# One block of a fused scan and feed-forward kernel moved from per-pair to joint processing

## The chip, the core and the metric

The kernel runs on one core of a Trainium2 chip. A core has five engines that run side by side and wait for each other through semaphores: TensorE (PE, matrix products; its weight loads are shown as PEld), VectorE (DVE), ScalarE (ACT), GpSimd (POOL) and SyncE (SP, which here only issues transfers). SP, ScalarE and GpSimd can each issue transfers (DMAs) between the device memory and the on-chip memory. TensorE writes to eight on-chip accumulator banks (PSUM); VectorE and ScalarE read them, GpSimd does not. The metric is the device time of the whole kernel in microseconds; lower is better.

## The reference

A state-space scan over 4 sequences of 768 tokens, 8 heads of 32 values and 16 states, and then a bilinear feed-forward of 3,072 tokens:

```
for each chunk of the sequence (log_a, cum: decay within the chunk)
    M = (C @ B^T) * exp(cum_i - cum_j) * causal       # per head, tokens by tokens
    y = M @ x  +  (C @ state) * exp(cum)              # within the chunk, and from before it
    state = decay * state + sum_j exp(cum_end - cum_j) * B_j x_j
X   = y laid out as (3072 tokens, 256)
out = ((X @ w_a) * (X @ w_b)) @ w_out                 # 256 -> 1536 -> 256
```

Inputs and outputs are float32; the kernel multiplies in float16 and accumulates in float32.

## The kernel before, in words

**Tiling.** The 768 tokens of a sequence are cut into 6 blocks of 128. The 4 sequences form 2 pairs, so there are 12 steps, called pair 0 to pair 11: pairs 0 and 1 are block 0, pairs 2 and 3 are block 1, and so on. A pair holds two sequences (`bt`), 256 tokens.

**One pair's scan.** Its B, C and x are loaded (`load1`, `load2`). `scale_bc` multiplies B and C by decay factors, `scale_x` scales x to float16. B and C are turned so that the state index lies on the partitions: for pairs 0 to 3 by TensorE (`transposes`, with copies BT by ScalarE and CT by VectorE), for later pairs by a transposing transfer (`turn`, which SP issues after GpSimd has filled `planes`). `scores` writes C times B into the four banks SC0 and SC1. `mask` multiplies each quarter by the causal triangle, on VectorE, or by way of a ScalarE copy `tmp` on GpSimd (`by_pool=True`). Then come the products with the incoming state (`Sbd`, made on GpSimd by `state_spread`), with x (`pv_u`), and the state sums (`ds_mm`), all in the SC banks again.

**Two forms of a block.** Pairs 0 to 3 run one by one: `pv` computes one pair's output into SC1 and copies it to `X2T`; its state product (line 492) takes the full, block-diagonal `sbd` of 128 x 512, spread with `maskbd`. From pair 4 on, a block runs jointly: `group` and `outputs` compute both pairs' outputs (state product at line 523 with the small `spair`), and three ScalarE copies (lines 551 and 553) write them to `XB`.

**Feed-forward.** A per-pair unit (`unit_mm`, line 616) covers two of the 12 slices of 128 hidden columns for 256 tokens: four matmuls of 256 columns into a bank for `aps`, four into a bank for `bps`. ScalarE copies aps to `asb` (`evac_a`, line 630), VectorE multiplies bps and asb (`times`, line 637). A joint unit (`bunit`, line 682) covers one slice for the 512 tokens of a block: two matmuls of 512 columns for each. The output product (`out_mm` at line 652, `bout` at line 709) takes 12 matmuls for each 128 tokens; ScalarE copies the result (`osb`), SP stores it.

**Order.** The order is written by hand (`manual_schedule`): each engine runs its instructions in the order of the Python calls, and so does each queue of transfers. In the built program a transfer also waits until the one eight places before it on the same issuer has landed. A matmul's first write to a bank waits until the bank's last reader is done. The feed-forward and output tiles share four banks; the string `BANKS` says which bank each tile takes, in order of the calls.

**Around the change.** GpSimd issues, one after another, the weight loads (`load_w`, `load_wo`) and some inputs of pairs 1 and 2; SP issues B, C and x of pair 3 after the second half of Wb has landed (`w1[1]`), then those of later pairs and the transposing loads. PE interleaves block 0's units with the scan of pairs 1, 2 and 3, then block 1's units pair by pair, and joins the joint form at block 2 (line 682 for the first time at 52.20 us).

Of the kernel before, what the change touches and what calls it, by code (L numbers as in the profile page):

```python
# [22 lines left out]
    "032130132013201320120310231023120132031203120132013201320310213021320310231023120130231023"  # L23
    "1021320312031203123021302130213021302130213021031203120312031203120312031203120312031"
# [4 lines left out]
def kernel(  # L29
# [26 lines left out]
    NG = NBLK - 1  # L56
    P0 = 4
# [10 lines left out]
    ph = np.zeros((128, H + 2), np.float32)  # L68
    ph[:, 0:H] = (j[:, None] // N) == np.arange(H)[None, :]
    ph[:, H:] = (j[:, None] // N) % 2 == np.arange(2)[None, :]  # L70
# [4 lines left out]
    ch = const.tile([128, H + 2], f32, name="ch")  # L75
# [5 lines left out]
    headm = ch[:, 0:H]  # L81
    par = ch[:, H:]
# [8 lines left out]
    X2T = big.tile([128, P0, 2, 2, Q], f16, name="X2T")  # L91
    XB = big.tile([128, NBLK - P0 // NBP, 2, 2, NBP, Q], f16, name="XB")
    U32 = big.tile([128, NP, 2, 2 * D], f32, name="U32")
    gU = big.tile([128, NP, 2, 2 * D], f32, name="gU")
    maskbd = big.tile([128, H, D], f16, name="maskbd")
# [92 lines left out]
    nc.sync.dma_start(ch, ph_t.ap())  # L188
# [240 lines left out]
    def pv_u(p, u, py, first):  # L429
# [12 lines left out]
        for r in range(2) if p < P2 else ():  # L442
            for g in range(4):
                for bt in range(2):
                    h = u * 4 + g
                    k = slice(64 * bt, 64 * bt + 64)
                    c0 = 32 * (g ^ 2 * bt) if p >= P0 else 32 * g
                    nc.tensor.matmul(  # L448
                        py[bt, u][c0 : c0 + 32] if p >= P0 else py[bt][c0 : c0 + 32, u * Q : (u + 1) * Q],
                        s["X16"][k, h, r, :],  # L450
                        s["T1"][k, h, r, :],
                        start=(first and u == 0 and r == 0),
                        stop=(r == 1),
                        skip_group_check=True,
                        tile_position=(64 * bt, c0),
                    )
# [28 lines left out]
    def pv(p, DS=None, split=False):  # L485
        blk, bp = divmod(p, NBP)
        s = st[p]
        PY = [SC1[:, bt, 0:256] for bt in range(2)]
        if blk > 0:
            for bt in range(2):  # L490
                for u in range(2):
                    nc.tensor.matmul(
                        PY[bt][:, u * Q : (u + 1) * Q],
                        s["Sbd"][:, bt, u * 128 : u * 128 + 128],
                        s["CT"][:, bt],
                        start=(u == 0),
                        stop=False,
                        skip_group_check=True,
                    )
        for u in range(2):  # L500
            pv_u(p, u, PY, blk == 0)
        if blk < NBLK - 1:
            ds_mm(p, *(DS or (256, SC[2:])))
        o_ = X2T[:, p].rearrange("p t u q -> p t (u q)")
        i_ = SC1[:, :, 0:256]
        if split:
            c0 = nc.scalar.activation(out=o_[:, 0], in_=i_[:, 0], func=AF.Copy, scale=YS / XS)
            c1 = nc.vector.tensor_scalar(o_[:, 1], i_[:, 1], YS / XS, None, ALU.mult)
            tc.declare_no_dep(c1.ins, c0.ins.name, reason="reads of two banks")
        else:  # L510
            nc.scalar.activation(out=o_, in_=i_, func=AF.Copy, scale=YS / XS)

    def outputs(blk):
# [29 lines left out]
        for bt, to, fr in ((0, whole, whole), (1, low, high), (1, high, low)):  # L543
            if blk == NBLK - 1:
                for j in range(NBP):
                    o_ = XB[to, blk - P0 // NBP, :, bt, j]
# [7 lines left out]
                out=XB[to, blk - P0 // NBP, :, bt].rearrange("p u j q -> p u (j q)"),  # L554
# [29 lines left out]
    def state_spread(p):  # L584
        blk, bp = divmod(p, NBP)
        if p + NBP < P0:
            Sbd = mid.tile([128, 2, H * D], f16, name="sbd", tag="sbd")
            nc.gpsimd.tensor_tensor(
                out=Sbd.rearrange("p t (m c) -> p t m c", m=4),
                in0=U32[:, p].unsqueeze(2).broadcast_to((128, 2, 4, 2 * D)),  # L590
                in1=maskbd.rearrange("p (m e) d -> p m (e d)", e=2).unsqueeze(1).broadcast_to((128, 2, 4, 2 * D)),
                op=ALU.mult,
            )
        else:
            Sbd = mid.tile([128, 2, 2 * D], f16, name="spair", tag="spair")
            nc.gpsimd.tensor_tensor(
                out=Sbd.rearrange("p t (e d) -> p t e d", e=2),
                in0=U32[:, p].rearrange("p t (e d) -> p t e d", e=2),
                in1=par.unsqueeze(1).unsqueeze(3).broadcast_to((128, 2, 2, D)),
                op=ALU.mult,  # L600
            )
# [72 lines left out]
    def bunit(blk, k):  # L674
# [4 lines left out]
        for W in (Wa, Wb):  # L679
            t_ = bank("aps" if W is Wa else "bps")  # L680
            for f in range(2):
# [5 lines left out]
                    XB[:, blk - P0 // NBP, f].rearrange("p t j q -> p (t j q)"),  # L687
# [12 lines left out]
    def bout(blk, c, parts=1):  # L700
# [4 lines left out]
        for part in range(parts):  # L705
# [16 lines left out]
            if blk * NBP < P2:  # L722
# [99 lines left out]
    for bt in range(2):  # L822
        load1(nc.gpsimd, 2, 1, bt)
    load_wo(0)
    nc.gpsimd.tensor_copy(maskbd, headm.unsqueeze(2).broadcast_to((128, H, D)))
    load_wo(1)
    tiles(3)
    for bt in range(2):
        load1(nc.gpsimd, 2, 2, bt)
    times(0, 0, bps[0], asb[0])  # L830
    pv(1, DS=(0, SC[:2]), split=True)
# [6 lines left out]
    for t_ in planes:  # L838
        nc.gpsimd.memset(t_[:, 0:4].bitcast(u32), 0)
    scale_bc(2, 1, nc.gpsimd)  # L840
    go((1, 0), (1, 1), (1, 2))
    state_sums(0)
    state_sums(1)
    state_spread(0)
    state_spread(1)
    b3 = [load1(nc.sync, 3, 0, bt) for bt in range(2)]
    tc.add_manual_dep(b3[0].ins, w1[1].ins.name, AFTER, reason="weights ahead of pair 3's inputs")
    for bt in range(2):
        load1(nc.sync, 3, 1, bt)
    loads_x(3, nc.sync)  # L850
    loads_bc(4)
    go((0, 3), (0, 4), (1, 3), (0, 5))
    transposes(2, apart=True)
    go((1, 4))
    h = unit(1, 5)
    scores(2)
    mask(product(2, 3), by_pool=True)
    mask(product(2, 0))
    mask(product(2, 1))
    mask(product(2, 2))  # L860
    h()
    scale_x(2, nc.scalar)
    scale_bc(3, 0, nc.gpsimd)
    scale_bc(3, 1, nc.gpsimd)
    scale_x(3, nc.gpsimd)
    loads_bc(5)
    o = [bank("ops"), bank("ops")]
    out_mm(0, 0, o[0], range(6))
    out_mm(0, 1, o[1], range(6))
    out_mm(0, 0, o[0], range(6, NK))  # L870
    out_store(0, 0, o[0])
    pull(2)
    pv(2, split=True)
    out_mm(0, 1, o[1], range(6, NK))
    out_store(0, 1, o[1])
    h = unit(2, 0, lambda: transposes(3, apart=True))
    state_sums(2)
    fb(2)
    h()
    h = unit(2, 1)  # L880
# [46 lines left out]
    scores(3)  # L927
    prep(4, (2,))
# [5 lines left out]
    mask(product(3, 0))  # L934
    h()
    for m in range(1, 4):
        mask(product(3, m))
    out_half(1, 0)
    out_half(1, 1)
    go((2, 2))  # L940
    pull(3)
    pv(3)
    state_sums(3)
    late_rows(nc.gpsimd)
    state_spread(3)
    nc.gpsimd.tensor_copy(
        causal_r.rearrange("p r (s i) -> p r s i", s=2), causal.rearrange("p r (i s) -> p r s i", s=2)
    )
    go((2, 3), (2, 4), (2, 5))
    late_factors()  # L950
    fb(3)
    out_half(2, 0)
    o_ps = bank("ops")
    out_mm(2, 1, o_ps, range(6))
# [5 lines left out]
    masked(4, (0, 1))  # L960
    out_mm(2, 1, o_ps, range(6, NK))
    out_store(2, 1, o_ps)
    masked(4, (2,), *pu(3, 0))
    go((3, 1))
    scale_x(5, nc.scalar)
# [105 lines left out]
```

## Time and profile before

| | |
|---|---|
| median of 3 runs | 125.04 us (124.65 to 125.16) |
| span of the profiled execution | 123.5 us; what lies around it, against the median, 1.5 us |
| TensorE busy | 117.6 us, 95% of the span |
| VectorE, ScalarE, GpSimd busy | 86.4, 71.9, 62.8 us |
| granted TensorE clock | 1.00 throughout |
| transfers | 13.74 MB |

Times in the text count from the start of the span. Busy PE includes overlapped matmuls, so the cost of a piece is taken from the start of one piece to the start of the next. "L616" is line 616 of the kernel before; a helper's line stands for all its calls.

### The profile page before, as it was taken

The page shows a single profiled execution, that of the slowest core. Times are in us where ns is not written, and L with a number is a line of the kernel's source. Part 1 is how long each engine was busy: PE and PEld are TensorE (multiplying, and loading weights), DVE is VectorE, ACT ScalarE, POOL GpSimd, SP SyncE. Part 2 cuts the span into 40 slices and gives each one's busy share as a digit, 9 for nine tenths or more (in the row PEclk, how much of TensorE's full clock was granted, in tenths as well). Part 3 has the DMA queues.
Part 4 walks back from the last instruction along what each step waited for, and adds up shares of the span by engine and source line. Part 5 has one row for each costly group of instructions (what it writes and reads, how often), then busy time and mean ns, then how long its engine had stood idle before and what let it go on. Part 6 is the DMA issues. An engine that isn't in the chain of part 4 may idle for free.

```text
span 123.5 us, 3874 instructions
## 1 busy us (share of the span) xinstructions
PE 117.6 (95%) x1527; PEld 79.8 (65%) x1527; DVE 86.4 (70%) x166; ACT 71.9 (58%) x142; POOL 62.8 (51%) x109
## 2 busy tenths in 40 slices
PE   5988999999999999899999999999999999999990
PEld 2445698978898788644467455756464784655880
DVE  1886889795968979298984989857899444847100
ACT  0465845866364795687758746664737736566220
POOL 7999999956873399089850895026900000000000
PEclk9999999999999999999999999999999999999999
DMA  3999999994659988697995973999541012010132
GB/s 64 154 163 237 171 196 181 194 145 74 99 115 185 92 83 147 84 120 79 134 155 74 150 264 87 70 95 161 113 130 42 5 42 85 0 42 0 48 101 69
DMA packets 60754, 13.74 MB, mean 111 GB/s; under 512 B 55632, under 2 KB 60400, under 8 KB 60736
## 3 DMA queue, kind: packets, MB, share of 16 engines
q1 hardware_dynamic: 56608, 9.53, 49.8%
q0 software_dynamic: 2128, 3.61, 16.3%
q10 hardware_dynamic: 2000, 0.36, 1.6%
q8 instruction: 12, 0.20, 0.7%
q14 instruction: 6, 0.05, 0.1%
HBM read 11.13 MB, written 3.15 MB: 116 GB/s over the span
## 4 chain that ended last, share of the span: by engine, by line
PE 83%; DMA 6%; POOL 5%; ACT 2%; issue 1%; DVE 1%; ACTq 0%; POOLq 0%
PE ops L709 18%; PE aps L682 17%; PE bps L682 17%; PE ops L652 9%; PE aps L616 8%; PE bps L616 7%; DMA xn<-in_x_dram 6%; PE SC L373 2%; PE SC L448 1%; PE SC L433 1%; PE SC L388 1%; POOL cn L154 1%; PE SC L523 1%; PE SC L475 1%; POOL bn L154 1%; POOL causal L214 1%
## 5 line engine op out<-in xcount | busy, mean ns | idle before, releaser
L630 ACT COPY asb<-aps 128x512 f32<-128x512 f32 x72 | 41.9, 587 | 14.8 <-PE aps L682 9.7
L694 DVE TENSOR_TENSOR hkb<-bps,asb 128x512 f16<-128x512 f32 x48 | 32.3, 689 | 12.9 <-ACT asb L630 11.7
L682 PE MATMUL aps<-XB,Wa 128*128 128x512 f16 x96 | 28.6, 379 | 0.0
L682 PE MATMUL bps<-XB,Wb 128*128 128x512 f16 x96 | 28.5, 379 | 0.0
L709 PE MATMUL ops<-Wo,hkb 128*128 128x256 f16 (+1 forms) x204 | 22.5, 267 | 0.0
L709 PEld LDWEIGHTS <-hkb 128*128 128x128 f16 x204 | 18.5, 98 | 3.1
L637 DVE TENSOR_TENSOR hk<-bps,asb 128x512 f16<-128x512 f32 x24 | 16.2, 688 | 2.9 <-ACT asb L630 2.4
L682 PEld LDWEIGHTS <-Wb 128*128 128x128 f16 x96 | 9.9, 103 | 11.0 <-issue 0.2
L427 DVE TENSOR_TENSOR t<-SC,causal_q 128x512 f16<-128x512 f32 x21 | 13.4, 682 | 3.9 <-PE SC L373 3.9
L682 PEld LDWEIGHTS <-Wa 128*128 128x128 f16 x96 | 9.7, 103 | 9.1 <-issue 0.4
L616 PE MATMUL aps<-X2T,Wa 128*128 128x256 f16 x96 | 14.3, 273 | 0.4 <-DMA Wa<-in_moe_w_a_dram 0.3
L721 ACT ACTIVATE osb<-ops 128x256 f32<-128x256 f32 (+1 forms) x16 | 6.0, 377 | 14.3 <-PE ops L709 14.2
L616 PE MATMUL bps<-X2T,Wb 128*128 128x256 f16 x96 | 14.3, 273 | 0.0
L652 PE MATMUL ops<-Wo,hk 128*128 128x256 f16 x96 | 11.6, 273 | 0.0
L616 PEld LDWEIGHTS <-Wa 128*128 128x128 f16 x96 | 9.5, 103 | 2.0 <-DMA Wa<-in_moe_w_a_dram 0.8
L616 PEld LDWEIGHTS <-Wb 128*128 128x128 f16 x96 | 9.7, 103 | 0.7
L652 PEld LDWEIGHTS <-hk 128*128 128x128 f16 x96 | 8.9, 98 | 1.5 <-DVE hk L637 0.2
L293 POOL TENSOR_SCALAR x<-xn 128x512 f16<-128x512 f32 x6 | 9.0, 1493 | 1.7 <-DMA xn<-in_x_dram 1.3
L427 DVE TENSOR_TENSOR t<-SC,causal 128x512 f16<-128x512 f32 x13 | 8.2, 684 | 1.4 <-PE SC L388 1.3
L304 POOL TENSOR_TENSOR planes<-cn,fCl 128x256 f16<-128x256 f32 x6 | 3.7, 622 | 8.1 <-DMA cn<-in_C_dram 8.1
L425 POOL TENSOR_TENSOR t<-tmp,causal_q 128x512 f16<-128x512 f32 x3 | 3.5, 1159 | 7.3 <-ACT tmp L424 7.2
L553 ACT ACTIVATE XB<-SC 64x512 f16<-64x512 f32 (+1 forms) x9 | 5.3, 594 | 2.9 <-PE SC L462 1.6
(102 smaller groups left out, 128.8 us busy)
## 6 DMA issues: line engine op xcount, KB each, us to landing
out_dram<-osb SPq DMA_DIRECT2D x19, 128.0 KB, 1.8
xn<-in_x_dram SPq DMA_DIRECT2D x5, 256.0 KB, 5.3
xn<-in_x_dram SPq DMA_DIRECT2D x7, 128.0 KB, 3.4
Wa<-in_moe_w_a_dram POOLq DMA_DIRECT2D x2, 384.0 KB, 6.2
Wb<-in_moe_w_b_dram POOLq DMA_DIRECT2D x2, 384.0 KB, 7.8
Wo<-in_moe_w_out_dram POOLq DMA_DIRECT2D x2, 384.0 KB, 6.8
cn<-in_C_dram SPq DMA_DIRECT2D x6, 128.0 KB, 4.2
bn<-in_B_dram SPq DMA_DIRECT2D x6, 128.0 KB, 4.3
```

Source lines behind the costliest of these rows:

```text
L293: eng.tensor_scalar(xo, xi, XS, None, ALU.mult)
L304: eng.tensor_tensor(out=planes[p % 2][:, 4:6].rearrange("p t (h n) -> p t h n", n=N), in0=raw, in1=f.unsqueeze(3).broadcast_to((128, 2, H, ...
L427: nc.vector.tensor_tensor(out=o_, in0=i_, in1=c_, op=ALU.mult)
L553: nc.scalar.activation(out=XB[to, blk - P0 // NBP, :, bt].rearrange("p u j q -> p u (j q)"), in_=SCt[bt][fr, :, 0 : NBP * Q], func=AF.Copy ...
L616: nc.tensor.matmul(ps[:, kk * 2 * Q : (kk + 1) * 2 * Q], W[k // 6][:, f, k % 6 // 3 * 384 : (k % 6 // 3 + 1) * 384].rearrange("p (c kk) -> ...
L630: (nc.vector.tensor_copy if on_dve else nc.scalar.copy)(asb, a_ps)
L637: nc.vector.tensor_tensor(out=s["hk"][:, 2 * k2 : 2 * k2 + 2, :].rearrange("p k q -> p (k q)"), in0=b_ps, in1=asb, op=ALU.mult)
L652: nc.tensor.matmul(o_ps[:, 0:d_model], hk[:, k, bt * Q : (bt + 1) * Q], Wo[:, k, :], start=(k == 0), stop=(k == NK - 1), skip_group_check= ...
L682: nc.tensor.matmul(t_, W[k // 6][:, f, k % 6 // 3 * 384 : (k % 6 // 3 + 1) * 384].rearrange("p (c kk) -> p kk c", kk=3)[:, k % 3], XB[:, b ...
L694: return lambda: nc.vector.tensor_tensor(out=s["hk"][:, k], in0=ps[1], in1=asb, op=ALU.mult)
L709: nc.tensor.matmul(o_ps[:, 0:w], hk[:, k, c * Q : (c + 1) * Q], Wo[:, k, cs], start=(k == 0), stop=(k == NK - 1), skip_group_check=True,)
L721: nc.scalar.activation(out=o_sb[:, 0:w], in_=o_ps[:, 0:w], func=AF.Copy, scale=1.0 / (YS * YS))
```

## The change

Block 1 takes the joint form. `X2T` keeps two pairs (`PJ = 2`), `XB` holds five blocks, and `pv` shrinks to `pv1` for pair 1 alone. The block-diagonal `sbd`, `maskbd` and the head mask constant go. Pairs 2 and 3 are scored and masked one after the other among the last units and first output products of block 0; then `group(1)`, the rest of block 0's output products, and 12 joint units of block 1 around the scores of pairs 4 and 5. B and C of pair 3 are issued by GpSimd ahead of both halves of `Wo`, x of pairs 2 and 3 by SP after Wb's second half; the second half of `Wo` is issued after pair 2's B and C are scaled. `planes` are cleared later. x of pair 3 is scaled by ScalarE instead of GpSimd. Block 1's masks use GpSimd three times (before once). The results of block 1 join the late stores of block 0. `BANKS` is new.

```diff
+    PJ = 2
-    X2T = big.tile([128, P0, 2, 2, Q], f16, name="X2T")
-    XB = big.tile([128, NBLK - P0 // NBP, 2, 2, NBP, Q], f16, name="XB")
+    X2T = big.tile([128, PJ, 2, 2, Q], f16, name="X2T")
+    XB = big.tile([128, NBLK - PJ // NBP, 2, 2, NBP, Q], f16, name="XB")
-    maskbd = big.tile([128, H, D], f16, name="maskbd")
...
-    def pv(p, DS=None, split=False):
+    def pv1():
...
     for bt in range(2):
         load1(nc.gpsimd, 2, 1, bt)
+    tiles(3)
+    for w in range(2):
+        for bt in range(2):
+            load1(nc.gpsimd, 3, w, bt)
     load_wo(0)
-    nc.gpsimd.tensor_copy(maskbd, headm.unsqueeze(2).broadcast_to((128, H, D)))
-    load_wo(1)
-    tiles(3)
-    for bt in range(2):
-        load1(nc.gpsimd, 2, 2, bt)
+    for p in (2, 3):
+        for x_ in load2(nc.sync, p, 2):
+            tc.add_manual_dep(x_.ins, w1[1].ins.name, AFTER, reason="weights ahead of x")
+    loads_bc(4)
     times(0, 0, bps[0], asb[0])
...
     scale_bc(2, 0, nc.gpsimd)
-    for t_ in planes:
-        nc.gpsimd.memset(t_[:, 0:4].bitcast(u32), 0)
     scale_bc(2, 1, nc.gpsimd)
+    load_wo(1)
+    scale_bc(3, 0, nc.gpsimd)
+    scale_bc(3, 1, nc.gpsimd)
     go((1, 0), (1, 1), (1, 2))
     state_sums(0)
     state_sums(1)
+    for t_ in planes:
+        nc.gpsimd.memset(t_[:, 0:4].bitcast(u32), 0)
     state_spread(0)
     state_spread(1)
...
-    go((0, 3), (0, 4), (1, 3), (0, 5))
+    go((0, 3), (0, 4), (1, 3))
     transposes(2, apart=True)
-    go((1, 4))
-    h = unit(1, 5)
-    scores(2)
+    fb(2)
+    go((0, 5))
+    h = unit(1, 4, lambda: scores(2))
+    h()
     mask(product(2, 3), by_pool=True)
     mask(product(2, 0))
+    h5 = unit(1, 5)
+    transposes(3, [bank("tb"), bank("tc")])
+    mask(product(2, 2), by_pool=True)
     mask(product(2, 1))
...
     o = [bank("ops"), bank("ops")]
     out_mm(0, 0, o[0], range(6))
     out_mm(0, 1, o[1], range(6))
+    h5()
+    scores(3)
+    mask(product(3, 3), by_pool=True)
+    for m in range(3):
+        mask(product(3, m))
+    scale_x(2, nc.scalar)
+    for bt in range(2):
+        o.append(bank("ops"))
+        out_mm(1, bt, o[-1], range(6))
     out_mm(0, 0, o[0], range(6, NK))
+    scale_x(3, nc.scalar)
     out_store(0, 0, o[0])
+    loads_bc(5)
+    late_rows(nc.gpsimd)
...
+    prep(4)
     loads_x(4, nc.sync)
     loads_x(5, nc.sync)
     prep(5)
     loads_bc(6)
     loads_bc(7)
+    group(1)
+    for c in range(1, 4):
+        p, bt = divmod(c, NBP)
+        out_mm(p, bt, o[c], range(6, NK))
+        out_store(p, bt, o[c])
+    state_spread(2)
+    state_spread(3)
     late_factors()
     fb(3)
+    bgo(1, 0, 1, 2, 3)
     scores(4)
     mask(product(4, 3), by_pool=True)
     scale_x(4, nc.scalar)
     prep(6)
+    for m in range(3):
+        mask(product(4, m))
+        bgo(1, *range(4 + 3 * m, min(7 + 3 * m, NK)))
     scores(5)
     mask(product(5, 3), by_pool=True)
+    scale_x(5, nc.scalar)
...
+    for m in range(3):
+        mask(product(5, m))
+    bout(1, 0)
+    bout(1, 1)
     group(2)
-    out_half(3, 0)
-    out_half(3, 1)
+    bout(1, 2)
+    bout(1, 3)
```

## The prediction, made before the changed kernel was run

> **What bounds the kernel now.** I read the page first: who is busy, and the chain that ended last.
>
> ```profile
> PE 117.6 (95%) x1527; PEld 79.8 (65%) x1527; DVE 86.4 (70%) x166; ACT 71.9 (58%) x142; POOL 62.8 (51%) x109
> PEclk9999999999999999999999999999999999999999
> PE 83%; DMA 6%; POOL 5%; ACT 2%; issue 1%; DVE 1%; ACTq 0%; POOLq 0%
> L682 PE MATMUL aps<-XB,Wa 128*128 128x512 f16 x96 | 28.6, 379 | 0.0
> L616 PE MATMUL aps<-X2T,Wa 128*128 128x256 f16 x96 | 14.3, 273 | 0.4 <-DMA Wa<-in_moe_w_a_dram 0.3
> ```
>
> TensorE is the bound, at the full clock. The 379 and 273 ns are pipelined durations; the price of a matmul is the step from one start to the next, which the chain of waits shows. So I took the chain next, over the stretch that the change rewrites.
>
> ```profile
> 18.85 0.59 ACT asb L630
> 19.47 0.70 DVE hk L637
> 20.21 0.60 PE aps L616 x4
> ...
> 22.55 0.44 PE bps L616 x4
> ...
> 27.39 0.32 PE SC L492 x4
> 27.71 0.35 PE SC L448 x32
> ...
> 47.49 0.25 PE SC L523 x16
> 47.74 0.65 PE SC L448 x62
> 48.39 0.26 PE SC L475 x29
> 48.65 2.74 PE ops L652 x24
> 51.41 0.39 ACT osb L664
> 51.88 0.40 PE SC L373 x14
> ```
>
> A half unit (four 256-column matmuls) takes 0.44. The chain leaves TensorE once, at 18.85, until a bank is free at 20.21, and again at 51.4. In between it never leaves it: a gain here is PE work removed, and any new wait comes straight off it. After 52 us the order of work on PE is the same in both kernels, so I compare when the scores of pair 6 start (51.30 by the timeline).
>
> Last, the loads and the ScalarE step that could become new waits (timeline, and the list of issues over windows of a single issue):
>
> ```profile
> Wo<-in_moe_w_out_dram POOLq DMA_DIRECT2D x1, 384.0 KB, 7.5
> xn<-in_x_dram SPq DMA_DIRECT2D x2, 128.0 KB, 3.2
> 33.22 1.32 SPq L356 DMA_TRANSPOSE turned<-planes  x1
> 34.72 2.71 SPq L154 DMA_DIRECT2D xn<-in_x_dram  x4
> 41.42 0.63 ACT L291 ACTIVATE x<-xn 128x512 f16<-128x512 f32 x1
> ```
>
> The scale of pair 4's x (41.42) found its x long landed. In the changed kernel it comes some 4 us earlier.
>
> **The bank table: -0.25.** In before the first aps of (0,4) should follow at 19.09 + 2 x 0.437 = 19.96 but starts at 20.21, because its bank is that of (1,2)'s bps, read by VectorE until 20.16. In the new table that unit's aps takes the bank of (1,2)'s aps, copied out by 19.44, and bps the other, wanted at 20.40. The stall goes; nothing else is late at that place.
>
> **PE work removed: -0.61.** The rows of block 2, which already runs jointly, price block 1.
> - Feed-forward: 24 half units of four 256-column matmuls at 0.437 become 24 of two 512-column matmuls at 0.4315 (52.20 to 112.7, steps of 0.43): -0.13. Twice the width at half the count is the same stream.
> - Incoming state: L492 costs 0.31 for each pair (27.33 to 27.64, 34.76 to 35.07), 0.62; L523 for both pairs 0.25 (47.42 to 47.67): -0.37.
> - Intra-block output and state sums: 0.51 for each pair (27.64 to 28.15, 35.07 to 35.58), 1.02; jointly 0.91 (47.67 to 48.58): -0.11.
> - Transposes, scores and 96 output matmuls keep number and size: 0.
>
> The Trainium skill's TensorE: Matmul & The Clock Gate, Back-to-back issue gap, gives about 131 ns as the sustained step of a 512-column matmul; the trace steps 216 ns. By the page the 48 matmuls would save a further 48 x 0.085 = 4.1; I go by the row.
>
> **Small stalls moved: -0.06.** Before's bank wait at 45.54 (0.16) is gone with the old order. A switch from output matmuls to 32-row products costs 0.10 (40.28 to 40.38), and there is one more. The ceiling of the gain is 0.25 + 0.61 + 0.06 = 0.92.
>
> **Where the new order waits.** I set the new order against measured steps, from (1,3)'s end at 21.70.
> - VectorE from 20.84 has three products, CT, a reciprocal, two products, a mask, CT, a mask, a product and three masks. At the steps of 0.59 to 0.61 in the rows at 31 to 32 us (0.41 for CT, 0.31 for the reciprocal) it ends at 29.0. PE, adding its pieces, wants the joint outputs at 29.2: 0. At the 0.69 mean of one instead, VectorE ends 0.9 later: the range of this term is 0 to +0.85.
> - The first output matmuls of block 0 need a bank that ScalarE empties at 25.25: +0.1.
> - Wo. GpSimd now issues pair 3's B and C first; by the built program the last of them waits for the second Wb half (landed 18.8; in before x of pair 2 waited there until 19.07). So Wo's first half is issued at 19.8 instead of 16.34. In before it landed at 22.4, 2.3 after the ring's previous load (20.1). With 256 KB more ahead of it (the same amount took 1.3 at 18.8 to 20.1) I get about 24 to 24.3; PE wants it at 25.3: 0. The other bound is the 7.5 from issue to landing of the second half in before: 27.3, +2.0. I lean to the first, since the 7.5 held a longer backlog. Wo's second half (issued 21.7, wanted 28.5) has more room.
> - x of pairs 2 and 3 by SP, behind Wb's landing. B of pair 3 had that slot and took 7.6 (landed 26.5), its C 27.3 to 27.8. The same slots carry twice the bytes now; x of pair 2 is wanted at 27.8, of pair 3 at 28.5. x of pair 3 in before landed at 29.5 as the last of the same total: 0, at worst +0.5 (landed at 29.5 it is scaled by 30.15, and the pair's products want it at 29.7). Behind them in SP's queue, C and B of pair 4 move up two places, so cover is not lost there.
> - GpSimd: masks of pairs 2 and 3 end about 29.0, then late_rows 0.78, causal_r 0.39 and pair 4's planes and copies 1.75: 31.9 (33.2 in before). The transposing load lands 3.4 later, 35.4; PE wants scores(4) at 36.0: 0.
> - **x of pair 4** is the term that binds. SP issues it after that transposing load: 31.95 + 2.1 for the second half's issue, + 3.2 to land = 37.3. ScalarE reaches its scale right after the mask copy of pair 4 (37.0), and behind it stand the copies of joint units 4 and 5, which free the banks for units 6 and 7. Scale 0.63 and copy 0.59: bank free at 38.55; PE wants it at 38.1, and the next bps 0.1 more: +0.55. If x is there already, ScalarE alone costs +0.16; if it takes the 4.7 that x of pair 3 took in before, 38.75 and +1.9. I take the 3.2 of the very same load in before.
> - The joint group's evacuations (3 x 0.6, from 30.45) end at 32.2, covered by 18 output matmuls (2.05) until 32.45: 0; without that cover 1.8.
> - The 0.35 between 51.53 and 51.88 in before has no cause I can see (the ScalarE writes it needs ended at 50.56). I leave it in place: 0, or -0.35.
> - The mask of state blocks (POOL L825, 0.43), the pv variants and the smaller constant lie off the path: 0. The late stores keep their queue place.
>
> **Sum.** -0.92 + 0.1 + 0.55 = -0.27. The profiled execution spans 123.5; the median of runs is 125.04, so 1.5 lies around the span and I carry it over. **Forecast 124.7**, no change that can be told: about 0.5% (0.63 us) is what a measurement here can tell.
>
> **Rivals.**
> - *All waits hidden:* x of pair 4 lands half a microsecond earlier and the hole at 51.5 goes too. For it: block 2 runs the same scheme with no such hole. Against: three queues (GpSimd, SP, ScalarE) have to be early together. 125.04 - 0.92 + 0.1 + 0.16 - 0.3 = 124.1.
> - *Wo late (the other side):* decides once Wo's first half lands after 25.3 + 0.9 = 26.2, as all that follows (scores(3), masks, group) shifts with it. For it: 3.4 us later issue, and x on SP competing. Against: no TensorE wait for Wo in before, 1 us of slack by the ring's rate. At 27.3: 124.7 + 2.0 = 126.7; at 26.5: 125.9.
> - *x of pair 4 later still, or VectorE at its mean:* with 4.7 to land 124.7 + 1.35 = 126.05; with VectorE 0.85 late, 125.5 as part is taken up by the x wait. For it: ScalarE and VectorE have no slack of more than 0.3 in that stretch.
> - *The skill's 131 ns:* 124.7 - 4.1 = 120.6. That page's rule has 192 rows of block 2 onwards against it.
>
> **Chances.** Forecast (within 0.63 of before) 0.38; all hidden 0.35; Wo late 0.13; x or VectorE late 0.13; the page's step 0.01. So faster 0.36, same 0.38, slower 0.26. The range leaves out the 126.7 and the 120.6 ends and a little of each tail: 123.9 to 126.0.
>
> **What would show it.** No wait at (0,4)'s first aps near 20; L492's 0.31 gone and L523 at 0.25 near 29 to 30; ScalarE idle before x of pair 4 with the load as its releaser, near 37, and an aps of joint unit 6 starting late. Scores of pair 6 near 51.0. The forecast is wrong if PE waits for Wo near 25, if the joint outputs start after 29.6, or if ScalarE meets x of pair 4 without waiting.

## The result, and the profile after

The changed kernel takes 126.33 us in the median of 22 runs (124.57 to 128.60), the kernel before 125.01 in 22 runs beside it (124.46 to 125.97). The ratio is 1.0063, 95% interval 1.0040 to 1.0086: about 0.8 us slower. The ratio leaves out the changed kernel's ten longest executions and the medians do not, so the two differ. The forecast was 124.7 (123.9 to 126.0); the median lies outside its range. By the ratio alone the time would be 125.8, inside it, so the account below goes by the waits and not by the time alone.

The profiled execution took 127.11 us with a span of 125.4. That is above the median, so its waits are on the large side. One of the experiments (x of pair 4 early) runs the same program up to 31.7 us and has a profiled execution of 125.78, with the same wait for Wo at 0.75 instead of 1.74; I use it where a size matters.

The page of the changed kernel, the lines that answer to those shown of before:

```profile
PE 117.5 (94%) x1487; PEld 74.7 (60%) x1487; DVE 85.3 (68%) x164; ACT 73.8 (59%) x145; POOL 61.7 (49%) x110
PE 74%; DMA 15%; ACT 3%; issue 2%; POOL 2%; DVE 1%; SPq 0%; ACTq 0%; POOLq 0%
L652 PE MATMUL aps<-XB,Wa 128*128 128x512 f16 x120 | 35.7, 380 | 0.4 <-ACT asb L600 0.4
```

TensorE has 40 instructions fewer, and transfers hold 15% of the chain that ended last instead of 6%. The chain over the stretch that was rewritten says which:

```profile
10.87 8.67 DMA Wb<-in_moe_w_b_dram
19.54 0.28 issue
19.82 0.43 POOL cn L150
20.26 0.24 issue
20.50 7.32 DMA Wo<-in_moe_w_out_dram
27.82 0.05 issue
27.87 1.48 PE ops L622 x12
...
31.98 0.25 PE SC L502 x16
...
36.78 3.44 DMA xn<-in_x_dram
...
40.83 0.57 ACT asb L600
41.41 0.04 issue
41.45 0.59 PE aps L652 x2
```

Three loads stand in it. Wb's second half lands at 19.54; only then does GpSimd issue the last piece of pair 3's C, and behind it, at 20.50, the first half of Wo, which lands 7.32 later. Then x of pair 4. TensorE's timeline and GpSimd's show the first place from the other side:

```profile
25.86 0.27 PE L330 MATMUL tc<-ident,cm 128*128 128x128 f16 x2
27.87 1.48 PE L622 MATMUL ops<-Wo,hk 128*128 128x256 f16 x12 [1.74 <-DMA Wo<-in_moe_w_out_dram]
```
```profile
19.82 0.68 POOL L150 DMA_DIRECT2D cn<-in_C_dram  x1 [1.26 <-DMA Wb<-in_moe_w_b_dram]
20.50 0.72 POOL L172 DMA_DIRECT2D Wo<-in_moe_w_out_dram  x1
```

The output matmuls of block 0 begin at 27.87 (25.25 before), behind a wait of 1.74 for Wo. Meanwhile the DMA engines were not full. The busy times by window, first of before, then of the changed kernel; the last two columns are the DMA share (the mean busy share of the 16 DMA engines, which reads a little over 1 where they are full) and GB/s:

```profile
18.50:21.00 2.50, 2.41 (x23) 2.12 (x22) 2.23 (x7) 1.43 (x4) 2.29 (x6) 1.00 1.08 178
21.00:24.00 3.00, 3.00 (x32) 2.85 (x30) 2.64 (x5) 2.35 (x6) 3.00 (x4) 1.00 1.15 204
```
```profile
18.50:21.00 2.50, 2.50 (x26) 2.33 (x24) 2.14 (x8) 1.68 (x4) 1.24 (x3) 1.00 0.39 80
21.00:24.00 3.00, 2.71 (x26) 2.06 (x23) 2.51 (x6) 2.07 (x5) 2.96 (x6) 1.00 0.85 146
```

From 18.5 to 24 the changed kernel moves 0.64 MB (2.5 x 80 + 3 x 146), before 1.06 MB (2.5 x 178 + 3 x 204). The 0.42 MB between them is more than half of Wo. When Wb has landed, next to nothing else is queued: GpSimd's next issue and SP's x both wait for that landing. Between 20 and 21 us the share is 0.12.

The second place is a step between joint units, on ScalarE and TensorE:

```profile
40.29 0.63 ACT L287 ACTIVATE x<-xn 128x512 f16<-128x512 f32 x1 [0.29 <-DMA xn<-in_x_dram]
```
```profile
40.48 0.59 PE L652 MATMUL bps<-XB,Wb 128*128 128x512 f16 x2
41.45 0.59 PE L652 MATMUL aps<-XB,Wa 128*128 128x512 f16 x2 [0.38 <-ACT asb L600]
```

From 40.48 the next step should be at 40.91; it comes at 41.45: 0.54 lost.

For the experiments I use three marks on TensorE: S, the start of the Wb half of unit (0,2), a place that both kernels share; O, the first output matmul; M, the first 512-token matmul of block 2. Behind M all kernels run alike (before 123.5 - 52.20 = 71.3, after 125.4 - 54.08 = 71.3).

| kernel | S | O | M | O - S | M - O |
|---|---|---|---|---|---|
| before | 16.01 | 25.25 | 52.20 | 9.24 | 26.95 |
| changed | 16.14 | 27.87 | 54.08 | 11.73 | 26.21 |

Behind the first output matmul the change saves 0.74, with the x wait still in it; ahead of it, it loses 2.5.

### The profile page after: what moved, and what is told of

Read it like the earlier page. It is cut to its first block, busy times and chain, and to the rows that moved or that the text cites. A ratio compares the mean times of both kernels' runs of the same rounds, so it can differ in the third digit from the quotient of the medians.

```text
span 125.4 us, 3795 instructions
## 1 busy us (share of the span) xinstructions
PE 117.5 (94%) x1487; PEld 74.7 (60%) x1487; DVE 85.3 (68%) x164; ACT 73.8 (59%) x145; POOL 61.7 (49%) x110
## 4 chain that ended last, share of the span: by engine, by line
PE 74%; DMA 15%; ACT 3%; issue 2%; POOL 2%; DVE 1%; SPq 0%; ACTq 0%; POOLq 0%
PE ops L679 22%; PE aps L652 19%; PE bps L652 19%; DMA Wb<-in_moe_w_b_dram 7%; DMA Wo<-in_moe_w_out_dram 6%; PE ops L622 4%; PE SC L222 3%; DMA xn<-in_x_dram 3%; PE SC L369 2%; PE SC L429 1%; PE SC L444 1%; PE SC L384 1%; PE SC L502 1%; ACT asb L600 1%; ACT XB L532 1%
## 5 line engine op out<-in xcount | busy, mean ns | idle before, releaser
L664 DVE TENSOR_TENSOR hkb<-bps,asb 128x512 f16<-128x512 f32 x60 | 40.4, 688 | 15.0 <-ACT asb L600 13.7
L652 PE MATMUL aps<-XB,Wa 128*128 128x512 f16 x120 | 35.7, 380 | 0.4 <-ACT asb L600 0.4
L652 PE MATMUL bps<-XB,Wb 128*128 128x512 f16 x120 | 35.7, 379 | 0.0
L652 PEld LDWEIGHTS <-Wb 128*128 128x128 f16 x120 | 12.4, 103 | 13.6 <-issue 0.2
L652 PEld LDWEIGHTS <-Wa 128*128 128x128 f16 x120 | 12.0, 103 | 12.2 <-issue 1.1
L607 DVE TENSOR_TENSOR hk<-bps,asb 128x512 f16<-128x512 f32 x12 | 8.1, 688 | 1.3 <-ACT asb L600 0.9
L420 ACT COPY tmp<-SC 128x512 f32<-128x512 f32 x10 | 5.9, 587 | 4.3 <-PE SC L384 4.0
L586 PE MATMUL aps<-X2T,Wa 128*128 128x256 f16 x48 | 7.1, 273 | 0.1
L586 PE MATMUL bps<-X2T,Wb 128*128 128x256 f16 x48 | 7.1, 274 | 0.0
L421 POOL TENSOR_TENSOR t<-tmp,causal 128x512 f16<-128x512 f32 x5 | 5.8, 1162 | 2.2 <-ACT tmp L420 2.2
```

The lines of the kernel that those rows point to most:

```text
L421: nc.gpsimd.tensor_tensor(out=o_, in0=tmp, in1=c_, op=ALU.mult)
L586: nc.tensor.matmul(ps[:, kk * 2 * Q : (kk + 1) * 2 * Q], W[k // 6][:, f, k % 6 // 3 * 384 : (k % 6 // 3 + 1) * 384].rearrange("p (c kk) -> ...
L607: nc.vector.tensor_tensor(out=s["hk"][:, 2 * k2 : 2 * k2 + 2, :].rearrange("p k q -> p (k q)"), in0=b_ps, in1=asb, op=ALU.mult)
L652: nc.tensor.matmul(t_, W[k // 6][:, f, k % 6 // 3 * 384 : (k % 6 // 3 + 1) * 384].rearrange("p (c kk) -> p kk c", kk=3)[:, k % 3], XB[:, b ...
L664: return lambda: nc.vector.tensor_tensor(out=s["hk"][:, k], in0=ps[1], in1=asb, op=ALU.mult)
```

## The experiments

Three theories stood against each other in turn. **A**: the joint form saves the TensorE work that was counted, but loads come late ahead of block 0's outputs; Wo's place in GpSimd's ring is the first suspect. **B**: the joint form saves nothing even where nothing is late. Later, when each load that was moved ahead had made another one late, A split in two: **C**, the loads come late because the DMA engines stand idle behind Wb; **D**, there are too many bytes for the time, in whatever order.

**Wo ahead of pair 3's B and C.**

```diff
     tiles(3)
+    load_wo(0)
     for w in range(2):
         for bt in range(2):
             load1(nc.gpsimd, 3, w, bt)
-    load_wo(0)
```

> The changed kernel with one edit: the first half of Wo goes back ahead of pair 3's B and C on GpSimd's ring; all else stays. Theory A (Wo is late): in the changed kernel's trace Wo's first half is issued at 20.5 and lands at 27.8, and PE stands from 26.0 to 27.9 for it. Here it is issued near 16.5, lands by 23, the wait of 1.9 is gone, and the span falls by 1.2 to 1.9 from the 125.4 of that trace. Rival B (the joint form itself is slow, by ScalarE's and VectorE's hand-overs): PE meets another wait of the same size a step later (the scores of pair 3, or the joint outputs) and the span stays within 0.5 of 125.4.

Measured: 128.52 (127.88 to 129.69, 4 runs), ratio to before 1.0249 (1.0173 to 1.0324): slower still. TensorE's timeline, GpSimd's, and the busy times of one window of this run; the third number from the end is the granted TensorE clock:

```profile
18.05 0.26 PE L471 MATMUL SC<-x,bm 64*32 64x64 f16 x17 [1.78 <-issue]
...
28.48 0.60 PE L586 MATMUL bps<-X2T,Wb 128*128 128x256 f16 x4
28.92 0.28 PE L330 MATMUL tb<-ident,bm 128*128 128x128 f16 x2
...
29.32 1.51 PE L622 MATMUL ops<-Wo,hk 128*128 128x256 f16 x12
```
```profile
24.79 0.61 POOL L308 TENSOR_TENSOR bm<-bn,fB 128x256 f16<-128x256 f32 x1 [2.30 <-DMA bn<-in_B_dram]
27.55 0.62 POOL L308 TENSOR_TENSOR cm<-cn,fC 128x256 f16<-128x256 f32 x1 [2.15 <-DMA cn<-in_C_dram]
```
```profile
18.50:21.00 2.50, 2.50 (x14) 1.80 (x12) 1.03 (x3) 0.58 (x1) 2.37 (x4) 0.50 0.94 154
```

Wo is issued at 16.99, lands 6.8 later, and TensorE never waits for it. Instead GpSimd waits 2.30 for pair 3's B and 2.15 for its C, so that C is scaled only by 28.17. In this execution no wait on TensorE comes of that, because TensorE itself is late: a hole of 1.78 inside one group of matmuls, for which the profile shows no releaser, and behind it a granted clock of 0.50 until about 21.9. Five half units take 3.87 there (18.24 to 22.11) instead of 2.18. These two make O 29.32, and the transposes of pair 3, at 28.92, follow the unit before them without a wait. Without the hole and the low clock TensorE would want them at about 25.5 (28.92 - 1.78 - 1.69), 2.7 before C is scaled; that is an estimate. Of the other three executions, which have no trace, two had a mean clock of 1.00 and took 127.88 and 129.69. That the late inputs of pair 3 made those slow is argued from the estimate, not shown. The last section comes back to the hole.

**x of pairs 2 and 3 held back until Wo's first half has landed.**

```diff
-    load_wo(0)
+    wo0 = load_wo(0)
...
-            tc.add_manual_dep(x_.ins, w1[1].ins.name, AFTER, reason="weights ahead of x")
+            tc.add_manual_dep(x_.ins, wo0.ins.name, AFTER, reason="weights ahead of x")
```

> The changed kernel with one edit: SP issues x of pairs 2 and 3 only when Wo's first half has landed, not when Wb's second half has. It tells what makes Wo late once it is issued at 20.5. Theory A1 (the x loads take bandwidth from it): Wo lands 2.3 to 3 after the ring's load before it, as in the kernel before, at 25 to 25.5 instead of 27.8, and PE waits at most 0.2 for it. Theory A2 (its place behind pair 3's B and C and the late issue alone): it lands within 0.5 of 27.8. In both, x of pairs 2 and 3 and all of SP's loads behind them come some 5 later, so the whole time gets longer, by 1 to 4; only the landing of Wo and PE's wait for it are read from this run.

Measured: 128.28 in one run. The two halves of Wo in the list of issues, and the list of waits:

```profile
Wo<-in_moe_w_out_dram POOLq DMA_DIRECT2D x1, 384.0 KB, 4.7
...
Wo<-in_moe_w_out_dram POOLq DMA_DIRECT2D x1, 384.0 KB, 5.8
```
```profile
ACT x L287 <- DMA xn<-in_x_dram: 3.1, 3, 1.3
```

Issued at 21.08, Wo's first half takes 4.7 instead of 7.3: SP's loads beside it (four of x, then C and B of pair 4) had taken 2.6 of its time. The Trainium skill's DMA: Bandwidth & Descriptors, Queues, rings and completion order, says that each DMA engine takes its queue rows in turn, packet by packet. The 4.7 against 7.3 agrees with such sharing. But now x is late three times.

**x of pair 3 alone held back, with x of pair 4 issued early.**

```diff
-    load_wo(0)
+    wo0 = load_wo(0)
...
-            tc.add_manual_dep(x_.ins, w1[1].ins.name, AFTER, reason="weights ahead of x")
+            tc.add_manual_dep(x_.ins, (w1[1] if p == 2 else wo0).ins.name, AFTER, reason="weights ahead of x")
...
-    prep(4)
     loads_x(4, nc.sync)
+    prep(4)
```

> The changed kernel with x of pair 4 issued early and x of pair 3 alone held back until Wo's first half has landed; x of pair 2 stays behind Wb. If Wo is late by the bandwidth that x takes, half the competing bytes take away about half of the delay: Wo lands at 26 to 27 and PE waits 0.5 to 1 for it. x of pair 3 then lands at 29.5 to 30.5, which the joint outputs want at 29 to 30, and pair 4's C and B come later. I expect 125.3 to 126.3, between the changed kernel and before; below before would be a surprise.

Measured: 127.42 (127.12 to 127.48, 4 runs), 1.0191 (1.0128 to 1.0254). TensorE's timeline:

```profile
26.91 1.27 PE L622 MATMUL ops<-Wo,hk 128*128 128x256 f16 x10 [0.79 <-DMA Wo<-in_moe_w_out_dram]
...
39.47 0.43 PE L384 MATMUL SC<-turned 32*64 32x128 f16 x32 [1.48 <-DMA turned<-planes]
```

Wo is still 0.79 late, and what stands behind x of pair 3 in SP's queue has slipped: the transposing load is issued at 36.30, and the scores of pair 4 wait 1.48 for it.

**x of pair 4 ahead of the transposing load.**

```diff
-    prep(4)
     loads_x(4, nc.sync)
+    prep(4)
```

> The changed kernel with one edit: SP issues x of pair 4 ahead of pair 4's transposing load instead of behind it. Theory C (x of pair 4 holds ScalarE, behind which the copies of joint units 4 and 5 stand): in the changed kernel PE waits 0.54 at joint unit 6 (41.45); here x lands before ScalarE gets to it, that wait falls to 0 to 0.2, and the span falls by 0.3 to 0.5, with the wait for Wo unchanged. Rival: ScalarE alone (mask copy, scale, copies in a row) is the limit, and the wait stays above 0.4.

Measured: 126.54 (125.34 to 126.90, 10 runs), 1.0081 (1.0036 to 1.0127), not below the changed kernel. TensorE's timeline:

```profile
27.09 0.39 PE L622 MATMUL ops<-Wo,hk 128*128 128x256 f16 x2 [0.75 <-DMA Wo<-in_moe_w_out_dram]
...
39.56 0.59 PE L652 MATMUL bps<-XB,Wb 128*128 128x512 f16 x2
40.14 0.59 PE L652 MATMUL aps<-XB,Wa 128*128 128x512 f16 x2
```

The step at the x wait is 0.58 instead of 0.97, and M - O is 25.68, 0.53 less than in the changed kernel; the time does not show it here. Wo is issued at 20.00, takes 7.0 and is 0.75 late, and S lies at 16.91; with S at 16.14 the same landing would have cost 1.5 (0.75 + 0.77).

**The change's transfers alone, in the kernel before**, with its computation as it was.

```diff
+    tiles(3)
+    for w in range(2):
+        for bt in range(2):
+            load1(nc.gpsimd, 3, w, bt)
     load_wo(0)
...
-    load_wo(1)
-    tiles(3)
-    for bt in range(2):
-        load1(nc.gpsimd, 2, 2, bt)
+    for p in (2, 3):
+        for x_ in load2(nc.sync, p, 2):
+            tc.add_manual_dep(x_.ins, w1[1].ins.name, AFTER, reason="weights ahead of x")
+    loads_bc(4)
...
     scale_bc(2, 1, nc.gpsimd)
+    load_wo(1)
...
-    b3 = [load1(nc.sync, 3, 0, bt) for bt in range(2)]
...
-        load1(nc.sync, 3, 1, bt)
-    loads_x(3, nc.sync)
-    loads_bc(4)
```

> The kernel before with only the transfers of the change: pair 3's B and C by GpSimd ahead of Wo, x of pairs 2 and 3 by SP behind Wb, the second half of Wo behind pair 2's scaling; computation and bank table as before. Theory A (the transfers alone cost it): PE reaches the first output matmuls at 25.25 and waits for Wo until 27 to 28, so the kernel is slower than before by 1.5 to 2.5, 126.5 to 127.5. Rival B (the joint form costs it): within 0.5 of before.

Measured: 129.99 (128.73 to 131.93, 4 runs), 1.0322 (1.0236 to 1.0407). TensorE's timeline:

```profile
27.92 1.48 PE L652 MATMUL ops<-Wo,hk 128*128 128x256 f16 x12 [2.27 <-DMA Wo<-in_moe_w_out_dram]
31.13 0.81 PE L652 MATMUL ops<-Wo,hk 128*128 128x256 f16 x6 [1.73 <-DMA Wo<-in_moe_w_out_dram]
```

The transfers by themselves cost about 4 us, more than was expected, as both halves of Wo are late. The joint form has other work between its output products, and there TensorE does not wait for the second half; so the whole change costs less than this part of it.

**The banks alone, in the kernel before.**

```diff
-    "032130132013201320120310231023120132031203120132013201320310213021320310231023120130231023"
+    "032130132013201320123013201320123102301230123102310231023013210321023013201320123103201320"
```

> The kernel before with one edit: from the unit (0,4) on, banks 0 and 3 change places in the table, so that this unit's aps takes a bank that is free. The prediction's step: PE no longer stands from 19.96 to 20.21, and the time falls by 0.25 (0.2%), at the edge of what can be told; in the trace aps of (0,4) starts 0.44 after bps of (0,3). Rival: VectorE, which is behind at this place, takes the 0.25 back before the scores of pair 2, and the time stays.

Measured: 124.99 (12 runs) beside 124.95, ratio 1.0008 (0.9987 to 1.0028). TensorE's timeline:

```profile
19.85 0.60 PE L616 MATMUL bps<-X2T,Wb 128*128 128x256 f16 x4
20.29 0.60 PE L616 MATMUL aps<-X2T,Wa 128*128 128x256 f16 x4
```

The step is 0.44, the stall of 0.25 is gone, and O - S is 9.03. The time shows nothing of it; a gain of 0.25 us would be 0.998, just outside the interval.

**The changed kernel with no need for Wo in block 0** (its output matmuls read a piece of Wa; Wo is still loaded), and the same with x of pair 4 early.

```diff
-                Wo[:, k, :],
+                Wa[0][:, 0, 0:d_model],
```

> The changed kernel with one edit: block 0's output products read a piece of Wa that is already there instead of Wo (block 0's result is then not the reference's); all transfers, Wo's too, stay as they are. It takes the need for Wo away and leaves the rest. Theory A (the joint form is cheaper, the late Wo costs more than it gains): no wait at the first output matmuls, they start at 25.4 to 26.2; what is left is the wait of 0.5 for x of pair 4, perhaps one for x of pair 3 of up to 0.8; the time is 0.1 to 0.7 below the kernel before, 1.2 to 2 below the changed kernel. Rival B (the joint form loses by itself): it stays above the kernel before by 0.3 or more.

> The run before (block 0's output products on a piece of Wa, so block 0's result is not the reference's) with x of pair 4 issued ahead of pair 4's transposing load as well. If the wait for x of pair 4 is a cost of its own, behind Wo's, this is 0.3 to 0.5 below the run without that edit, and 0.5 to 1.1 below the kernel before: the 0.92 that the prediction counted as the joint form's ceiling, less hand-overs. If not, the two are equal.

Measured: 125.32 (124.36 to 125.78, 12 runs), 1.0020 (0.9988 to 1.0051); with x early 125.31 (124.47 to 126.35, 12 runs), 1.0027 (0.9995 to 1.0059). The loss is gone, but no gain takes its place, which by the expectation would speak for B. TensorE's timeline of the first shows another late load:

```profile
21.40 0.29 PE L330 MATMUL SC<-ident,bm 128*128 128x128 f16 x2
22.74 0.28 PE L330 MATMUL SC<-ident,cm 128*128 128x128 f16 x2 [1.06 <-POOL cm L308]
```

The next load stands in line: GpSimd scales C of pair 2 at 22.07 after a wait of 0.72 for its landing, and its transposes come 1.2 late. In the second run Wb's second half is 0.58 late as well.

**Both kernels with less to load.** Block 0's outputs read Wa in both, and pair 3 uses pair 2's B and C, so that 256 KB are not loaded; every engine does the work that it did. Then two further profiled executions of the lightened joint kernel. In the joint kernel, besides block 0's outputs:

```diff
-    raw = by_token(pair_in[p][which]) if p >= P2 else pair_in[p][which].rearrange("p h r n -> p r h n")
+    raw = by_token(pair_in[p][which]) if p >= P2 else pair_in[2 if p == 3 else p][which].rearrange("p h r n -> p r h n")
...
-    for w in range(2):
-        for bt in range(2):
-            load1(nc.gpsimd, 3, w, bt)
```

> The changed kernel with less to load: block 0's output matmuls read a piece of Wa instead of Wo, and B and C of pair 3 are not loaded at all (pair 3 uses pair 2's B and C), so its results are not the reference's; the work of every engine is the same. To be compared with the kernel before, lightened in the same way (the next run). Theory A (the joint form saves the 0.9 us of TensorE work and small stalls that were counted, and late transfers in the first 30 us take it back): 0.5 to 1.0 us below the lightened kernel before, thus 123.8 to 124.5 if that one is at 124.8, pair 2's C in time (transposes of pair 2 at 21.5, not 22.7) and the first output matmuls at about 25.3. Rival B (the saving never existed in time, since between the output matmuls and the fused block another engine sets the end): within 0.3 us of the lightened kernel before.

> The kernel before with less to load: block 0's output matmuls read a piece of Wa instead of Wo, B and C of pair 3 are not loaded (pair 3 uses pair 2's), so its results are not the reference's. Control for the run above. Both theories: the kernel before waits for neither transfer (Wo lands at 22.4, pair 3's inputs are not waited for), so 124.6 to 125.1, the same as the kernel before; a lower time would mean that transfers slow the old form as well.

> The lightened joint kernel again, for a second profiled execution, since its executions lie between 123.97 and 125.66 us and the profiled one took 124.27 with the first 512-token matmul of block 2 at 51.29. Block 0's output matmuls read a piece of Wa and pair 3's B and C are pair 2's, so its results are not the reference's. Theory A (late transfers of single executions make the spread): when its time is above 124.9, that matmul comes at 51.7 or later, behind a named transfer, and the stretch behind it is again 71.2 us. Rival B (the spread arises behind block 1, or in the clock): that matmul at 51.3 whatever the time, and the stretch behind it longer by the difference.

> The same once more, for a third profiled execution; the same two theories. A time near 124.3 should then show the first 512-token matmul of block 2 at 51.2 to 51.5 and a stretch of 71.2 us behind it by both.

Measured: the joint kernel 124.82 (123.97 to 125.66, 12 runs), 1.0006 (0.9975 to 1.0037); the kernel before, lightened, 124.53 (123.98 to 124.99, 12 runs), 0.9964 (0.9942 to 0.9987). By the times B is right: the joint kernel is not faster than the other. And the kernel before, when lightened, came out below the 124.6 that was expected at the least; by that expectation the transfers slow the old form as well. The marks of the profiled executions say otherwise than B:

| kernel | time | S | O | M | O - S | M - O |
|---|---|---|---|---|---|---|
| before, banks moved | 125.05 | 16.34 | 25.37 | 52.02 | 9.03 | 26.65 |
| before, lightened | 124.66 | 15.77 | 25.01 | 51.83 | 9.24 | 26.82 |
| joint, Wo not needed | 125.41 | 15.62 | 26.36 | 52.39 | 10.74 | 26.03 |
| joint, lightened | 124.27 | 15.77 | 25.18 | 51.22 | 9.41 | 26.04 |
| the same, second execution | 124.77 | 15.61 | 25.58 | 51.73 | 9.97 | 26.15 |
| the same, third execution | 124.56 | 15.77 | 25.57 | 51.53 | 9.80 | 25.96 |

Behind O the joint form is 0.5 to 0.9 shorter than the kernels of before in this table (the lightened one has a wait of 0.36 for x of pair 2 in it). Ahead of O, with no wait, it takes 9.41, 0.17 more than before, as the transposes of pair 3 (0.40) now stand there and the bank stall (0.25) is gone. So by the marks B falls; by the time it falls only in the last group of runs. The spread of the three executions arises ahead of O, where C of pair 2 or Wb's second half is late by some tenths, as was expected under A; behind M they run 71.3, 71.4 and 71.4. The x wait is still in this kernel (0.5 in the first execution), and the run cannot tell C from D: with pair 3's inputs gone, Wo is issued earlier too, and the DMA share at 18.5 to 21 is 1.04.

**Filling the idle stretch.** GpSimd's ring holds pair 3's B and then Wo; C of pair 3 goes by SP as soon as Wa's second half has landed. The last runs add x of pair 4 early, release SP's x by Wa instead of Wb, or both.

```diff
-    for w in range(2):
-        for bt in range(2):
-            load1(nc.gpsimd, 3, w, bt)
+    for bt in range(2):
+        load1(nc.gpsimd, 3, 0, bt)
     load_wo(0)
+    for bt in range(2):
+        c_ = load1(nc.sync, 3, 1, bt)
+        tc.add_manual_dep(c_.ins, w1[0].ins.name, AFTER, reason="Wa ahead of pair 3's C")
```

> The changed kernel with GpSimd's ring holding pair 3's B, then Wo's first half, and pair 3's C by SP once Wa's second half has landed (17.6). Theory C (the loss comes from the idle DMA engines between 18.5 and 21 us, as the issue behind pair 3's first C piece waits for Wb's landing): Wo is issued at about 17.9 instead of 20.5, the engines are 0.8 busy or more at 18.5 to 21, Wo lands by 25, output matmuls at 25.3 to 26.0, the time 124.6 to 125.4. Rival D (too many bytes for the time): Wb's second half, C of pair 3 or x comes late by what Wo gains, output matmuls at 26.5 or later, time 126 to 127.

> The same with x of pair 4 issued ahead of the transposing load. Theory C: 0.2 to 0.5 below the run above, thus 124.2 to 125.0, which would be below the kernel before. Rival D: as the run above, 126 to 127.

> The changed kernel with one line other: SP's x of pairs 2 and 3 wait for Wa's second half (17.6) instead of Wb's (19.5); Wo stays behind pair 3's C. Theory C: the engines are 0.8 busy or more at 18.5 to 21, part of x is through when Wo is issued at 20.5 or a little later, which then lands 5 to 6 behind its issue instead of 7.3; output matmuls at 26 to 26.8, the time 125.2 to 125.9. Rival D: Wb's second half lands 0.5 to 1 later with it, so the gain is taken back: 126 to 126.8.

> All three: Wo ahead of pair 3's C, C and x released by Wa's landing, x of pair 4 early. Theory C: with 18.5 to 21 filled by e14's order already, no further gain: within 0.3 us of e15. Rival D: slower than e15 by 0.5 or more, as Wb's second half comes late.

| kernel | median (runs) | ratio to before | DMA share, 18.5 to 21 | O | M - O |
|---|---|---|---|---|---|
| Wo ahead of C | 125.31 (12) | 1.0037 (1.0006 to 1.0069) | 0.82 | 25.64 | 27.00 |
| and x of pair 4 early | 124.52 (12) | 0.9967 (0.9939 to 0.9995) | 1.16 | 25.52 | 25.94 |
| only x released by Wa | 126.48 (6) | 1.0115 (1.0079 to 1.0150) | 1.01 | 26.96 | 26.76 |
| all three | 124.52 (12) | 0.9970 (0.9947 to 0.9994) | 0.80 | 25.96 | 25.93 |

The second of them, by windows, on GpSimd and on TensorE:

```profile
18.50:21.00 2.50, 2.50 (x25) 2.36 (x24) 2.21 (x7) 1.68 (x4) 0.66 (x2) 1.00 1.16 146
```
```profile
17.81 0.74 POOL L172 DMA_DIRECT2D Wo<-in_moe_w_out_dram  x1
```
```profile
25.26 0.27 PE L330 MATMUL tc<-ident,cm 128*128 128x128 f16 x2
25.52 0.71 PE L622 MATMUL ops<-Wo,hk 128*128 128x256 f16 x5
...
38.26 0.59 PE L652 MATMUL bps<-XB,Wb 128*128 128x512 f16 x2
38.84 0.59 PE L652 MATMUL aps<-XB,Wa 128*128 128x512 f16 x2
```

C holds: the same bytes fit. Wo is issued at 17.81, lands 6.7 later at 24.5, TensorE waits for no load between S and O, and M - S is 35.43 against 36.19 in before (0.35 of that is a hole in that one execution of before, see below). This version is 0.3% (0.05 to 0.6%) below the kernel before, and about 1% below the changed one by the two ratios (0.9967 to 1.0063). The third run shows that filling the stretch is not enough: with x in it (wanted at 28), Wb's second half is 0.43 late, C of pair 3 is waited for until 25.80, and Wo, issued at 20.76, still lands late. D holds for that order alone. So filling the stretch helps when Wo is in it, and not as such. Wo ahead of C has a price too: in the traces of the first and the fourth run Wb's second half is 0.30 and 0.76 late.

The step from the first run to the second, 0.79 us, is the x wait of pair 4. With Wo in time TensorE loses 1.25 there in the profiled execution (38.33 to 40.01, less the 0.43 of a step); ScalarE waits 0.94 for x. TensorE's timeline of the first:

```profile
38.33 0.59 PE L652 MATMUL bps<-XB,Wb 128*128 128x512 f16 x2
40.01 0.59 PE L652 MATMUL aps<-XB,Wa 128*128 128x512 f16 x2 [1.08 <-ACT asb L600]
```

## Why the prediction was wrong

**The step that failed is "Wo: 0".** It put the landing at 24 to 24.3, wanted at 25.3; measured 27.8, and 27.05 in the quicker execution. The prediction let the ring drain on: the landing in before plus the time of 256 KB more. But its own point, that an issue now waits for Wb's landing, means that the ring runs dry there, and then the time counts from the issue. The rows for that overlap in all orders: 6.1 for the first half in before, 7.3 and 7.0 here, 7.5 with the transfers alone, 6.1 and 7.2 with Wo not needed, 5.8 to 6.9 in the runs that issued it early, and 4.7 only with all of SP's x held back. With the predicted issue at 19.8 (measured 20.50), rows of 5.8 to 7.5 give 25.6 to 27.3, all behind the 25.3 at which it is wanted. The bound of 7.5 that the prediction named, and set aside as the row of a longer backlog, was near the right one. The rival "Wo late", which had a chance of 0.13, is what happened: 126.7 at a landing of 27.3, against a median of 126.33.

**The forecast looked at each load against its own queue** and at GpSimd's wait only for what stands behind it there. SP's x waits for the same landing, so both queues were empty together: 0.39 of the DMA engines busy at 18.5 to 21. The profile of before could not show this (its share there is 1.08), but the prediction names both waits and does not put them side by side.

**The TensorE terms were right in the main.** A half unit steps 0.43 and the state product 0.25, as forecast. Output and state sums take 1.00 in the changed kernel (32.16 to 33.16) and 0.91 in the version that won, where 0.91 was forecast. One term was put at 0 and is not: the transposes of pair 3 take 0.22 in before (29.26 to 29.48) and 0.40 in the joint form. M - O falls by 0.91 from before to the first execution of the lightened joint kernel. The prediction's terms give -0.22 (pair 3's transposes now ahead of O) - 0.61 - 0.06 - 0.35 (the hole at 51.5) + 0.50 (the x wait there) = -0.74; the rest, some 0.2, is not explained. The step of 216 ns for a 512-column matmul held. The Trainium skill gives 131 ns for it (TensorE: Matmul & The Clock Gate, Back-to-back issue gap); no row here shows that.

**x of pair 4** was right in kind and place, but that its size came out is luck. In the changed kernel ScalarE came 0.29 ahead of x (0.3 forecast) and TensorE lost 0.54 (0.55 forecast). The 0.55 was forecast for Wo in time, and with Wo in time (the run with Wo ahead of C) TensorE lost 1.25. Against that run, the late Wo had put TensorE's joint units back by 2.1 (35.25 against 33.11) and the transposing load ahead of x by only 1.2 (34.61 against 33.40), so x caught up. The 33.40 is itself behind the 31.95 of the forecast, and x was scaled at 38.86 instead of 37.3. So even with Wo in time the kernel took 125.31, not 124.7.

**The bank table** does what was said at its place (19.65 to 20.09 is 0.44) and is worth nothing that the time shows.

**Covered as predicted:** VectorE ahead of the joint outputs, the group's evacuations (the last ends before 35.2, the next matmul is at 35.25), and the transposing load, which lost its cover only where x of pair 3 was held back.

**The 0.35 hole at 51.5** belongs to that one execution of before; it is not in the two variants of it above. The version that won (124.52) lies between the forecast and the rival "all hidden", 124.1, but only after two loads were moved; the change as it stood could not reach either. (The forecast's own sum, 125.04 - 0.27, is 124.77.)

**Still open:** why the changed kernel spreads more from run to run than before (124.57 to 128.60 against 124.46 to 125.97). A part is when Wo lands: 27.8 in the trace of 127.11, 27.05 in that of 125.78. The longest execution, 128.60, need not be the change's: its mean granted clock was 0.987, and the kernel before has executions of 127.86, 128.05 and 129.10 beside the experiments, at 0.985 to 0.987. None of these has a trace; the one traced execution with such a clock is that of the first experiment (128.66 at 0.987).

## What to carry to other kernels

When a change makes an issue wait for a landing, look at what is queued at that moment on every ring; if nothing is, the DMA engines stand idle and the next load counts from its issue, with the issue-to-landing row of the trace, not from the ring's rate. Read the DMA share of that stretch by window, before and after. And fill it with what is wanted first: with the weights there and one more load moved the same kernel was 1% faster, and with an input there that had time it was no faster (126.48 against 126.33).

## What the hardware showed that was not expected

- Issue to landing of a 384 KB load by GpSimd depended little on when it was issued (5.8 to 6.9 for Wo's first half issued between 16.2 and 18.1, 6.1 to 7.5 issued between 19.9 and 20.8, with other loads in flight), but fell to 4.7 when SP's ring was kept empty beside it.
- The transfers of the change cost more with the old computation (129.99) than with the new (126.33): this fits a late landing that hurts less where other work stands between the parts that need it.
- A hole of 1.78 between two matmuls of one group in the first experiment (16.27 to 18.05), with nothing in the profile that released it, and behind it a granted clock of 0.50 from 18.5 to about 21.9. TensorE's waits of 1.74 in the changed kernel and of 2.27 and 1.73 in the run with the transfers alone left the granted clock at 1.00. A 16 KB instruction fetch lay just ahead of the hole (15.6), some 3 us later than in before and in the changed kernel. But two executions of the lightened joint kernel have holes of 0.19 and 0.21 at the same place of the program, with that fetch at 12.5 as in before. The cause stays open.
